# Constant products on TensorE in the first microseconds, and mask copies moved behind the casts of unit 7

## The chip, the cores and the metric

The kernel runs on one core of one Trainium2 chip. The metric is the device time of one execution in microseconds (us): the median over three runs. A separate execution was recorded by the hardware profiler; its span is the time from the first to the last instruction, and the remainder of its device time lies around that span.

## The reference

Windowed attention with four sink keys, followed by a two-layer block with a gated activation. There are 4 batches, 8 heads, 768 positions and 64 elements per head.

```python
scores = scale * np.matmul(q, k.transpose(0, 1, 3, 2))
is_sink = pos[None, :] < 4
in_window = (rel >= 0) & (rel < 128)          # rel = query - key
scores = np.where(is_sink | in_window, scores, -1e9)
a = softmax(scores)                           # over the keys
attn = np.matmul(a, v)
...
x = attn.transpose(0, 2, 1, 3).reshape(3072, 512)
h = x @ w_in                                  # 512 -> 2048
g = h * (1.0 / (1.0 + np.exp(-beta * h)))
return g @ w_out                              # 2048 -> 512
```

## The kernel before

**Units.** The attention is cut into 32 units. Unit n is one batch (n // 8), one pair of heads (n % 4) and one half of the sequence, 384 queries (n // 4 % 2). Four units in a row make one tile T of 384 tokens of `xT`, the input of the second part, transposed. A unit goes through these steps:

- its q, k and v are loaded as f32 into `stage` (function `load`; DMA issues on SyncE's queue, lines 379 and 390, for v of units 0 and 1 on ScalarE's);
- `cast` (lines 425 and 428) copies them to bf16 on GpSimd: q and k into one of three buffers `qk16`, v into `v_aug`, whose buffer is shared by units that are eight apart, with one part for each half;
- for units below 12, `transpose_in` (line 447) has TensorE transpose q and k, six products of 128x128, into a PSUM bank, and ScalarE or VectorE copies that to `qkT` (line 454). From unit 12 on a transposing DMA does it;
- `scores` (line 487) multiplies keys and queries into PSUM in two parts; ScalarE takes the exponential of each part into `E` (line 493); VectorE multiplies it with a mask of zeros and ones (`mask`, line 502). From unit 12 on the two parts are handled at once (lines 521, 528, and 537, which reads the tile `mask_all`);
- `attend` (lines 560 and 571) multiplies with v, `normalise` (lines 579 and 581) divides, and `transpose_out` (line 598, and the copy on line 602) puts the result into `xT`; for units below 12 on TensorE.

**The second part.** `hidden(i)`, i from 0 to 127 (tile T = i // 16, block m = i % 16 of 128 columns of `w_in`), makes four products of 128x384 (line 618), a tanh on ScalarE (line 626) and a gate on VectorE (line 639). `project` (line 646) multiplies the gated tile with `w_out`, in products of 128x512, and the results leave by ScalarE, SyncE's queue and DMA. The weights come in 16 pieces of 512 KB (`load_w`, line 409), which GpSimd casts to bf16 (`cast_w`, line 414).

**The order.** The program is first written down as a list of operations with what each reads and writes (`op`). `Prog.order` then places them: each operation has a planned duration `busy` and a planned delay `lag` until others see its result, and on each engine the operation comes next that could start first by that plan, the earlier written one among equals. At most 160 places ahead of the first unplaced operation of an engine are looked at. `emit` derives the semaphore waits from the order. On the chip each engine works through its list in that fixed order: an operation that has to wait holds everything behind it on its engine. The plan holds no slower start of TensorE: a product of n columns is planned at 2.5 + n / 2.4 ns.

**The start.** `constants` fills tiles: `ones` on VectorE, the identity and the masks `mask_a` and `mask_b` on GpSimd, zeros in `v_sink` on VectorE. Units 0 to 3 are then written one after the other (lines 692 to 701): `enter(n)` (transposes, the cast of unit n + 2, and in `enter(1)` also the casts of weight pieces 0 to 3 and two small DMA issues on GpSimd for the sink rows of v, line 689), scores, masks, `attend`, `normalise`, and `transpose_out` through PSUM bank `acc1`. After that come the first three products of `hidden(0)` and `hidden(1)`, into `acc0` and `acc1`, `transpose_out(3)`, and a loop over steps s from -6, in which hidden blocks are written among the steps of units 4 and up (`FIRST` gives each unit's first step).

**The masks that units from 12 on use.** `mask_all` is filled by six copies on GpSimd, written at step s = 16 (lines 763 to 773). They read only `mask_a` and `mask_b`, which are there early, so the plan is free to place them early. The cast of unit 7 is written at step s = -3.

Of the kernel before, what the change touches and what calls it, by code (L numbers as in the profile page):

```python
# [49 lines left out]
class Node:  # L50


    __slots__ = ("id", "eng", "items", "busy", "lag", "preds", "succs", "open", "ready", "done",
                 "place", "dma")

    def __init__(self, id, eng):
        self.id, self.eng = id, eng
        self.items = []
        self.busy = self.lag = 0.0
        self.preds = {}  # L60
        self.succs = []
        self.open = 0
        self.ready = self.done = 0.0
        self.place = None
        self.dma = None


class Prog:

# [28 lines left out]

        return Together()

    def op(self, eng, fn, r=(), w=(), x=(), dma=None, busy=100.0, lag=None, behind=None):
        if self.group is not None and self.group.eng == eng:
            node = self.group
        else:
            node = Node(len(self.nodes), eng)
            self.nodes.append(node)
        events = []

        def dep(ev, raw):
            if ev is None or ev[0] is node:
                return
            same = ev[0].eng == eng and ev[0].dma is None and dma is None
            node.preds[ev[0].id] = ev[0]
            if not same or (raw and eng != "pe"):
                events.append(ev)

        for t in r:
            dep(self.writer.get(t), True)  # L120
        for t in (*w, *x):
            dep(self.writer.get(t), False)
            for ev in self.readers.get(t, ()):
                dep(ev, False)
        if behind is not None:
            events.append((node, behind))
        me = (node, len(node.items))
        if dma is not None:
            self.dma_count[dma] = self.dma_count.get(dma, 0) + 16
            node.dma = (dma, self.dma_count[dma])  # L130
        node.items.append((fn, dma, events))
        node.busy += busy
        node.lag = busy if lag is None else lag
        for t in r:
            self.readers.setdefault(t, []).append(me)
        for t in (*w, *x):
            self.writer[t] = me
            self.readers[t] = []

    def order(self):  # L140

        for n in self.nodes:
            n.open = len(n.preds)
            for p in n.preds.values():
                p.succs.append(n)
        free = dict.fromkeys(self.ENGINES, 0.0)
        left = {e: [n for n in self.nodes if n.eng == e] for e in self.ENGINES}
        head = dict.fromkeys(self.ENGINES, 0)
        can = {e: [n for n in left[e] if n.open == 0] for e in self.ENGINES}
        placed = []  # L150
        dma_free = self.FIRST_DMA

        def best(e):
            q = left[e]
            while head[e] < len(q) and q[head[e]].place is not None:
                head[e] += 1
            if head[e] == len(q):
                return None
            last = q[min(head[e] + self.AHEAD[e], len(q) - 1)].id
            c = [n for n in can[e] if n.id <= last]  # L160
            if not c:
                return None
            n = min(c, key=lambda n: (max(n.ready, free[e]), n.id))
            return max(n.ready, free[e]), n

        while len(placed) < len(self.nodes):
            found = [(*b, e) for e in self.ENGINES if (b := best(e)) is not None]
            start, n, e = min(found, key=lambda f: (f[0], f[1].id))
            free[e] = start + n.busy
            if n.dma is None:  # L170
                n.done = start + n.busy + n.lag
            else:

                dma_free = max(dma_free, start + n.busy) + n.lag
                n.done = dma_free + 2000.0
            n.place = start
            can[e].remove(n)
            placed.append(n)
            for s in n.succs:
                s.open -= 1  # L180
                s.ready = max(s.ready, n.done if s.eng != e or n.dma else start + n.busy)
                if s.open == 0:
                    can[s.eng].append(s)
        return placed
# [64 lines left out]
def bass_streamingllm_window__then__act_swish_beta_kernel(  # L249
# [21 lines left out]
    def sb(name, shape, dtype):  # L271
        ctx.append(nc.sbuf_tensor(name, list(shape), dtype))
        return ctx[-1].__enter__()

    def ps(name, shape, dtype):
        ctx.append(nc.psum_tensor(name, list(shape), dtype))
        return ctx[-1].__enter__()
# [8 lines left out]
    ones = sb("ones", (128, 256), BF16)  # L286
# [6 lines left out]
    mask_all = sb("mask_all", (128, 2, 768), BF16)  # L293
    stage = {t: [sb(f"{t}_stage{z}", (128, 2, 6, D), F32) for z in range(4)] for t in "qkv"}
    qk16 = [sb(f"qk16_{z}", (128, 2, 3, 2, D), BF16) for z in range(NQK)]
    v_aug = [sb(f"v_aug{z}", (128, 6, 2, D1), BF16) for z in range(4)]
# [13 lines left out]
    acc = [ps(f"acc{z}", (128, NOUT), F32) for z in range(2)]  # L310
# [3 lines left out]
    op = P.op  # L314
# [5 lines left out]
    def act(n):  # L320
        return {"busy": 80.0 + 0.81 * n, "lag": 140.0}
# [43 lines left out]
    MASK_A, MASK_B = ["mask_a", "mask_a1"], ["mask_b0", "mask_b1"]  # L365


    def place(n):

        return n // 8, n % 4, n // 4 % 2, n % 4  # L370
# [108 lines left out]
    def scores(n, c, bank, name):  # L479
        _, _, half, pb = place(n)  # L480
        at = 0
        with P.together("pe"):
            for kb, qb, nq in CHUNKS[half][c]:
                w = 128 * nq
                for hh in range(2):
                    rows = slice(64 * hh, 64 * hh + 64)
                    op("pe", lambda e, at=at, w=w, kb=kb, qb=qb, hh=hh, rows=rows: e.matmul(  # L487
                        bank[:, hh, at:at + w], qkT[pb][rows, kb // 3, 1, kb % 3 * 128:kb % 3 * 128 + 128],
                        qkT[pb][rows, half, 0, qb % 3 * 128:qb % 3 * 128 + w], start=True, stop=True),
                       r=[("qkT", pb, half), ("qkT", pb, kb // 3)], w=[f"{name}{hh}"],  # L490
                       busy=50.0 + w / 4.8, lag=260.0)
                at += w
        op("act", lambda e: e.activation(E[n % 2][:, c, :, 0:at], bank[:, 0:2, 0:at], AF.Exp,  # L493
                                         bias=0.0, scale=SCALE),
           x=[f"{name}0", f"{name}1"], w=[("E", n % 2, c)], **act(768))
# [170 lines left out]
    for n in range(4):  # L666
        load(n, "act" if n < 2 else "sp")
    op("act", lambda e: e.dma_start(beta_stage[:, :], moe_beta.rearrange("(m p) -> m p", p=128)),
       w=["beta_stage"], dma="beta")
# [6 lines left out]
    cast(0)  # L676
    cast(1)

    def enter(n):
        transpose_in(n, *((tr_ps, "tr") if n % 2 == 0 else (acc[0], "acc0")), "act")  # L680
        if n + 2 < 6:
            cast(n + 2)
        if n == 1:
            for i in range(4):
                cast_w(i)
            for hh in range(2):
                rows = slice(HEAD1 * hh, HEAD1 * hh + NSINK)
                s = v[:, :, 0:NSINK, :].rearrange("b (g h) s d -> s h (b g) d", h=2)[:, hh]
                op("gp", lambda e, hh=hh, rows=rows, s=s: e.dma_start(v_sink[rows, :, hh, 0:D], s),
                   w=[("v_sink", hh)], r=["v_sink"], dma=f"s{hh}")  # L690

    for n in range(4):
        enter(n)
        scores(n, 0, s_ps, "s")
        scores(n, 1, h_ps, "h")
        mask(n, 0)
        mask(n, 1)
        attend(n)
        normalise(n)
        if n < 3:  # L700
            transpose_out(n, acc[1], "acc1", "act" if n else "dve")
    op("pe", lambda e: nc.tensor.transpose(acc[0][:, 0:16], beta_stage[:, :], ident32[0:16, 0:16]),
       r=["beta_stage", "ident32"], w=["acc0"])
    op("dve", lambda e: e.tensor_scalar(beta_half[:, :], acc[0][:, 0:16], 0.5, None, ALU.mult),
       x=["acc0"], w=["beta"])
# [11 lines left out]
    for s in range(-6, S_END + NM):  # L717
# [5 lines left out]
        for n, step in here:  # L723
            half = place(n)[2]
# [20 lines left out]
        if s in casts:  # L745
            n = casts[s]
# [16 lines left out]
        if s == NM:  # L763

            first = {0: (mask_a[:, :], MASK_A), 1: (mask_b[:, 128:512], MASK_B)}
            for half in range(2):
                op("gp", lambda e, half=half: e.tensor_copy(mask_all[:, half, 0:TT], first[half][0]),
                   r=first[half][1], w=[("mask_all", half, 0)], busy=300.0)
                for x, n in ((0, 1), (1, 2)):
                    at = TT + 128 * x  # L770
                    op("gp", lambda e, half=half, n=n, at=at: e.tensor_copy(
                        mask_all[:, half, at:at + 128 * n], mask_b[:, 0:128 * n]),
                       r=MASK_B, w=[("mask_all", half, 1)], busy=200.0)
        if s == FIRST[7] + 1:

            for x in (8, 9, 10, 11):
# [61 lines left out]
```

## Time and profile before

| what | value |
|---|---|
| time, median of three runs | 240.41 us (239.73 to 241.25) |
| the profiled execution, device time | 241.05 us |
| its span | 239.3 us |
| TensorE products, busy | 217.9 us, 1677 instructions |
| TensorE weight loads, busy | 118.2 us |
| VectorE, busy | 137.7 us |
| ScalarE, busy | 147.7 us |
| GpSimd, busy | 73.3 us |
| read from HBM, written to it | 27.30 MB, 6.29 MB |

In the profile PE is TensorE's products, PEld its weight loads, DVE is VectorE, ACT is ScalarE, POOL is GpSimd, SP is SyncE; a q behind an engine's name is its instruction queue, where DMAs are issued. A row of the timeline has its start and its length in us, the engine, the line of the kernel, the operation, the tiles written and read, their shapes and the number of instructions merged into the row; in brackets the idle time before it and what ended it. A product's recorded duration holds the time of passing through the array: products overlap, and the distance between two starts is what one costs in a row of many. The chain of waits is the work that ended last, followed back from the last instruction.

### The profile page before, as it was taken

What the parts mean: (1) busy time and instruction counts of PE and PEld (TensorE: products, weight loads), DVE (VectorE), ACT (ScalarE), POOL (GpSimd) and SP (SyncE); (2) the same over time, 40 slices, a digit from 0 to 9 for tenths busy, and PEclk for the clock granted to TensorE, in tenths of its full rate; (3) what the DMA queues carried; (4) which work ended last, traced back from release to release, by engine and by line L of the source; (5) the groups of instructions that cost most, each with busy time, mean ns of one, the idle gap of its engine ahead of it and who ended that gap; (6) DMA issues with size and microseconds to landing.
All of it is one profiled execution on the core that took longest, in us unless ns stands there. A gap on an engine that the chain in (4) does not pass through costs nothing.

```text
span 239.3 us, 4359 instructions
## 1 busy us (share of the span) xinstructions
PE 217.9 (91%) x1677; PEld 118.2 (49%) x1677; DVE 137.7 (58%) x262; ACT 147.7 (62%) x254; POOL 73.3 (31%) x134
## 2 busy tenths in 40 slices
PE   0567769799999999999999999999999999999994
PEld 0244435455545555554555555555555555555441
DVE  4066499859974565653676537664666656434300
ACT  2477487559852756765877667658767865554411
POOL 7989568529251133232223337000000000000000
PEclk9999999999999999999999999999999999999999
DMA  7999999899799999999999976512201022111022
GB/s 176 260 374 280 334 377 294 221 284 251 169 227 207 209 183 276 231 164 216 225 167 237 195 148 152 126 28 60 63 16 47 16 60 63 44 44 44 5 85 88
DMA packets 96084, 39.76 MB, mean 166 GB/s; under 512 B 82736, under 2 KB 88896, under 8 KB 96064
## 3 DMA queue, kind: packets, MB, share of 16 engines
q1 hardware_dynamic: 93888, 39.07, 71.0%
q10 hardware_dynamic: 1632, 0.40, 0.8%
q8 instruction: 13, 0.21, 0.4%
q0 software_dynamic: 544, 0.02, 0.2%
q14 instruction: 7, 0.06, 0.1%
HBM read 27.30 MB, written 6.29 MB: 140 GB/s over the span
## 4 chain that ended last, share of the span: by engine, by line
PE 81%; DVE 11%; ACT 4%; POOL 2%; issue 1%; ACTq 0%
PE acc L646 34%; PE h_ps L618 28%; PE s_ps L571 5%; DVE E L502 5%; PE acc L618 4%; PE s_ps L521 4%; ACT E L493 2%; DVE g L639 2%; DVE qkT L454 1%; PE h_ps L646 1%; PE s_ps L487 1%; PE s_ps L560 1%; DVE v_sink L335 1%; PE s_ps L469 1%; DVE o_norm L581 1%
## 5 line engine op out<-in xcount | busy, mean ns | idle before, releaser
L646 PE MATMUL acc<-w_out,g 128*128 128x512 bf16 x368 | 98.5, 380 | 0.0
L626 ACT ACTIVATE th<-h_ps,beta_half 128x384 f32<-128x384 f32 x104 | 59.3, 582 | 39.0 <-PE h_ps L618 37.6
L618 PE MATMUL h_ps<-xT,w_in 128*128 128x384 bf16 x416 | 80.1, 326 | 0.2 <-DVE g L639 0.2
L639 DVE SCALAR_TENSOR_TENSOR g<-th,h_ps 128x384 bf16<-128x384 f32 x104 | 56.3, 552 | 33.3 <-ACT th L626 31.9
L618 PEld LDWEIGHTS h_ps<-xT,w_in 128*128 128x128 bf16 x416 | 39.6, 98 | 30.9 <-DVE g L639 1.7
L646 PEld LDWEIGHTS acc<-w_out,g 128*128 128x128 bf16 x368 | 34.4, 98 | 33.4 <-issue 3.0
L537 DVE TENSOR_TENSOR E<-E,mask_all 128x1536 bf16<-128x1536 bf16 x20 | 19.7, 984 | 26.4 <-ACT E L528 26.4
L528 ACT ACTIVATE E<-s_ps 128x1536 bf16<-128x1536 f32 x20 | 29.0, 1449 | 7.5 <-PE s_ps L521 7.1
L425 POOL CAST qk<-q_stage 128x384 bf16<-128x384 f32 x32 | 18.8, 588 | 34.2 <-DMA qkT<-qk 17.9
L428 POOL CAST v_aug<-v_stage 128x384 bf16<-128x384 f32 x32 | 17.1, 546 | 36.8 <-PE s_ps L571 35.9
L571 PE MATMUL s_ps<-v_aug,E 128*128 128x65 bf16 x384 | 21.1, 199 | 3.2 <-DVE E L502 3.0
L571 PEld LDWEIGHTS s_ps<-v_aug,E 128*128 128x128 bf16 x384 | 18.1, 101 | 9.0 <-DVE E L502 4.1
L618 PE MATMUL acc<-xT,w_in 128*128 128x384 bf16 x96 | 20.2, 341 | 1.6 <-DVE g L639 1.3
L654 ACT ACTIVATE out_sb<-acc 128x512 f32<-128x512 f32 x23 | 13.6, 597 | 11.3 <-PE acc L646 10.8
L581 DVE TENSOR_TENSOR o_norm<-s_ps,rden 128x384 bf16<-128x384 f32 x32 | 17.8, 558 | 1.8
L626 ACT ACTIVATE th<-acc,beta_half 128x384 f32<-128x384 f32 x24 | 13.8, 585 | 7.9 <-PE acc L618 7.4
L425 POOL CAST qk<-k_stage 128x384 bf16<-128x384 f32 x32 | 17.6, 550 | 0.1
L493 ACT ACTIVATE E<-s_ps 128x768 bf16<-128x768 f32 x16 | 13.0, 812 | 4.9 <-PE s_ps L487 4.7
L639 DVE SCALAR_TENSOR_TENSOR g<-th,acc 128x384 bf16<-128x384 f32 x24 | 13.0, 548 | 2.8 <-ACT th L626 2.7
L447 PE MATMUL s_ps<-ident,qk 128*128 128x128 bf16 x60 | 6.3, 246 | 8.8 <-POOL qk L425 8.3
L502 DVE TENSOR_TENSOR E<-E,mask_b 128x768 bf16<-128x768 bf16 x16 | 13.5, 847 | 1.2 <-ACT E L493 0.9
L618 PEld LDWEIGHTS acc<-xT,w_in 128*128 128x128 bf16 x96 | 8.4, 102 | 8.0 <-DVE g L639 3.5
(58 smaller groups left out, 147.4 us busy)
## 6 DMA issues: line engine op xcount, KB each, us to landing
out_dram<-out_sb SPq DMA_DIRECT2D x24, 256.0 KB, 2.7
q_stage<-in_q_dram SPq DMA_DIRECT2D x28, 192.0 KB, 4.3
k_stage<-in_k_dram SPq DMA_DIRECT2D x28, 192.0 KB, 4.9
wst<-in_moe_w_in_dram SPq DMA_DIRECT2D x8, 512.0 KB, 6.8
wst<-in_moe_w_out_dram SPq DMA_DIRECT2D x8, 512.0 KB, 7.6
v_stage<-in_v_dram SPq DMA_DIRECT2D x16, 192.0 KB, 4.0
v_stage<-in_v_dram SPq DMA_DIRECT2D x28, 96.0 KB, 5.0
q_stage<-in_q_dram SPq DMA_DIRECT2D x8, 96.0 KB, 4.1
```

What stands on the lines that cost most here:

```text
L425: op("gp", lambda e, x=x, name=name: e.tensor_copy(qk16[z][:, x, :, :, :], view(name)), r=[(name + "_stage", pb, half, hh) for hh in range ...
L428: op("gp", lambda e: e.tensor_copy(v_aug[pb][:, 3 * half:3 * half + 3, :, 0:D], view("v")), r=[("v_stage", pb, half, hh) for hh in range(2 ...
L493: op("act", lambda e: e.activation(E[n % 2][:, c, :, 0:at], bank[:, 0:2, 0:at], AF.Exp, bias=0.0, scale=SCALE), x=[f"{name}0", f"{name}1"] ...
L502: op("dve", lambda e: e.tensor_tensor(E[n % 2][:, c, :, 0:w], E[n % 2][:, c, :, 0:w], m[:, first:first + w].unsqueeze(1).to_broadcast([128 ...
L528: op("act", lambda e: e.activation(E[z][:, :, :, :].rearrange("p c h x -> p c (h x)"), s_ps[:, :, :].rearrange("p (h b) x -> p h (b x)", h ...
L537: op("dve", lambda e: e.tensor_tensor(both, both, mask_all[:, half, :].unsqueeze(1).to_broadcast([128, 2, 768]), ALU.mult), r=[("E", z, 0) ...
L571: last=(x == len(kbs) - 1): e.matmul(av_ps[:, at + hh * D1:at + hh * D1 + D1], E[z][:, c, h2, col:col + 128], v_aug[pb][:, kb, hh, :], sta ...
L581: op("dve", lambda e: e.tensor_tensor(o_norm[o][:, :, :, :].rearrange("p m h d -> p (m h) d"), src[:, :, 0:D], rden[z][:, :].unsqueeze(2). ...
L618: op("pe", lambda e: e.matmul(bank, w_in16[:, c, m * 128:(m + 1) * 128], xT[:, c, T * TT:(T + 1) * TT], start=(c == 0), stop=(c == 3)), r= ...
L626: op("act", lambda e: e.activation(th[i % 3][:, :], bank, AF.Tanh, bias=0.0, scale=beta_half[:, m:m + 1]), x=[name], r=["beta"], w=[("th", ...
L639: op("dve", lambda e: e.scalar_tensor_tensor(g[T % 2][:, m, :], th[i % 3][:, :], 1.0, bank, ALU.add, ALU.mult), r=[("th", i % 3)], x=[name ...
L646: op("pe", lambda e: e.matmul(bank, g[T % 2][:, m, t * 128:(t + 1) * 128], w_out16[:, m, :], start=(m == 0), stop=(m == NM - 1)), r=[("g", ...
```

## The change

Four things are changed.

1. `keep_busy(count, busy, behind)` is new. It writes `count` products of `ones` with `ones` (weights 128x128, 256 columns) into PSUM bank `acc1`; nobody reads them. Fourteen are written before unit 0 and wait for `ones` alone. Behind the transposes of unit 0, seven more read the cast k of unit 0 and seven the cast k of unit 1, so that they wait for these casts. Three follow each `transpose_out` of units 0, 1 and 2. That makes 37 products.
2. Because they write `acc1`, they stand in one order with the other users of that bank: `transpose_out` of units 0 to 2 comes after the products written before it, the three products behind it come after the copy that empties the bank, and so does `hidden(1)`.
3. An operation can carry `give`: in the choice of the next operation on an engine it counts as that much later. The constant products carry 200 ns. Their planned durations are 215, 200, 160 and 120 ns.
4. The six copies into `mask_all` also read v of unit 7 as cast (`("v_aug", 3, 1)`), so that they stand behind that cast on GpSimd.

```diff
-    def op(self, eng, fn, r=(), w=(), x=(), dma=None, busy=100.0, lag=None, behind=None):
+    def op(self, eng, fn, r=(), w=(), x=(), dma=None, busy=100.0, lag=None, behind=None,
+           give=0.0):
...
         node.busy += busy
+        node.give = give
...
-            n = min(c, key=lambda n: (max(n.ready, free[e]), n.id))
+            n = min(c, key=lambda n: (max(n.ready, free[e]) + n.give, n.id))
             return max(n.ready, free[e]), n
...
     cast(0)
     cast(1)
 
+    def keep_busy(count, busy, behind=()):
+
+        for _ in range(count):
+            op("pe", lambda e: e.matmul(acc[1][:, 0:256], ones[:, 0:128], ones[:, :], start=True,
+                                        stop=True), r=["ones", *behind], w=["acc1"], busy=busy,
+               lag=260.0, give=200.0)
+
+
+    keep_busy(14, 215.0)
...
     for n in range(4):
         enter(n)
+        if n == 0:
+            keep_busy(7, 200.0, [("k16", 0)])
+            keep_busy(7, 160.0, [("k16", 1)])
         scores(n, 0, s_ps, "s")
...
             transpose_out(n, acc[1], "acc1", "act" if n else "dve")
+            keep_busy(3, 120.0)
...
             for half in range(2):
                 op("gp", lambda e, half=half: e.tensor_copy(mask_all[:, half, 0:TT], first[half][0]),
-                   r=first[half][1], w=[("mask_all", half, 0)], busy=300.0)
+                   r=[*first[half][1], ("v_aug", 3, 1)], w=[("mask_all", half, 0)], busy=300.0)
                 for x, n in ((0, 1), (1, 2)):
...
-                       r=MASK_B, w=[("mask_all", half, 1)], busy=200.0)
+                       r=[*MASK_B, ("v_aug", 3, 1)], w=[("mask_all", half, 1)], busy=200.0)
```

More of the change, by code (lines that the diff above doesn't have):

```diff
@@ L50 @@
 class Node:
-    __slots__ = ("id", "eng", "items", "busy", "lag", "preds", "succs", "open", "ready", "done",
+    __slots__ = ("id", "eng", "give", "items", "busy", "lag", "preds", "succs", "open", "ready", "done",
                  "place", "dma")
@@ L58, in __init__ @@
         self.items = []
-        self.busy = self.lag = 0.0
+        self.busy = self.lag = self.give = 0.0
         self.preds = {}
```

## The prediction

> **What bounds the kernel now.** I read the page first, then the windows by stage, the chain of waits, and the timelines of GpSimd and TensorE. From the page, the chain that ended last:
>
> ```profile
> span 239.3 us, 4359 instructions
> ...
> PE 81%; DVE 11%; ACT 4%; POOL 2%; issue 1%; ACTq 0%
> ```
>
> TensorE carries it, but not all the way. The windows (columns: length, then busy time and instructions of PE, PEld, DVE, ACT and POOL, clock, DMA share, GB/s) show two regimes:
>
> ```profile
> 27.60:45.00 17.40, 13.34 (x144) 7.43 (x142) 15.64 (x28) 13.67 (x24) 13.80 (x20) 1.00 1.00 314
> 45.00:60.00 15.00, 13.98 (x114) 7.99 (x114) 12.03 (x24) 10.26 (x22) 8.14 (x11) 1.00 1.05 265
> ...
> 65.00:236.00 171.00, 170.98 (x1264) 90.73 (x1262) 93.27 (x174) 105.59 (x175) 28.45 (x56) 1.00 0.63 126
> ```
>
> From 65 us on TensorE never stops, so the end lies a fixed amount of TensorE work behind that point. Whatever brings the first 65 us forward brings the end forward; the change touches only these. The start is a serial walk through units 0 to 3, on GpSimd first (timeline of POOL):
>
> ```profile
> 4.28 1.37 POOL L689 DMA_DIRECT2D v_sink<-in_v_dram  x2 [0.83 <-DVE v_sink L335]
> 5.64 0.52 POOL L767 COPY mask_all<-mask_a 128x384 bf16<-128x384 bf16 x1
> ...
> 7.12 0.63 POOL L771 COPY mask_all<-mask_b 128x128 bf16<-128x128 bf16 x2
> 7.71 0.50 POOL L425 CAST qk<-q_stage 128x384 bf16<-128x384 f32 x1
> ```
>
> The first cast starts at 7.71, right behind the mask copies, though its q, issued at 0.81, landed 3.1 us later, at 3.9. TensorE's first product follows at 8.26. And early products are slow (timeline of PE):
>
> ```profile
> 23.78 2.11 PE L618 MATMUL acc<-xT,w_in 128*128 128x384 bf16 x6
> ...
> 26.78 0.82 PE L447 MATMUL s_ps<-ident,qk 128*128 128x128 bf16 x6 [0.57 <-ACT xT L602]
> ...
> 29.19 0.51 PE L447 MATMUL s_ps<-ident,qk 128*128 128x128 bf16 x6
> 29.54 0.81 PE L618 MATMUL acc<-xT,w_in 128*128 128x384 bf16 x4
> ```
>
> Six transposes take 0.82 us at 26.78 and 0.51 at 29.19; in the chain six products of line 618 take 1.92 us at 23.97 (320 ns each), later four take 0.65 (162 ns). TensorE runs at half speed until about 27.6, although the clock column reads 1.00 throughout: the column doesn't show it, the durations do.
>
> **Masks.** Removed from before cast 0: six copies, 5.64 to 7.71, 2.07 us. What was queued behind them is the row of casts of units 0 to 3, all issued back to back until 13.8. By issue plus time to landing, q and k of unit 0 are there at 3.9 and 4.9, of unit 1 at 6.1 and 7.3 (its v at 8.1), of unit 2 at 8.3 and 8.8 (v 9.8), of unit 3 at 11.5 and 12.2 (v 13.0). So unit 0 gains 2.07, unit 1 1.9, unit 2 1.5, unit 3 nothing. That is enough: the chain reaches unit 3's transposes only at 15.5, 2.8 us after its k can be cast, and the shift at unit 0 is handed on through exponentials and masks (11.50, 15.52, 19.44, 21.23). I count 2.07; bounds 1.5 (unit 2's data) and 2.07.
>
> The copies land behind the cast of unit 7 (27.42 to 28.8), ahead of the casts of weight pieces 4 to 7 (28.78 on, each waiting 0.2 to 0.8 for its data). Those move by up to 2.1 us. Piece 4 serves block 8, which the chain starts at 42.6, so this is free unless the start gains more than 8 us. Nothing is issued to SyncE's queue from there but loads into freed weight buffers, which have 10 us and more of slack (the last w_out piece lands at 56.8, is used after 75). Units 12 on need the masks at about 90. The price is company for VectorE: a masking of 128x768 took 0.56 us at 15.52 and 1.20 at 11.50, with casts on GpSimd. Two microseconds of copies in a stretch where VectorE is 90% busy cost 0 to 0.6 (one masking drawn out from 0.56 to 1.20); I take 0.3. Maskings at 9 to 11 us may get that back, as GpSimd then waits for data.
>
> **The clock.** The trace of before has no product before 8.26, so when the speed rises is to be bounded. Two stretches give a clue. In 23.06 to 26.0 TensorE streamed almost without a break (12 small products at 54 ns, six at 320, three at 107: 2.9 us) and was fast from 27.6. In 15.2 to 23 it was busy some three quarters of the time by the records, which hold latency, and stayed slow. After 27.6 waits of up to 1.1 us (at 35.37) did not slow it again. Fourteen constant products at 213 ns (320 x 256/384) are 2.98 us, from about 1.3 (when `ones` is written) to 4.3, as dense as the stretch that worked. Should they not suffice, unit 0's transposes at 6.2 with two times seven more products make the stretch from 6.2 to about 10 dense again. Value: fast from 6 to 10 us. Bounds: fast at unit 0's first step, or as late as before, at 27.6.
>
> [...]
>
> Worth, from rows of the chain between 8 and 27.6, slow against fast: three transposes of unit 1, 0.50 to 0.34; scores of unit 0, 0.51 to 0.34; `attend` of units 0 and 1, 0.68 to about 0.40 each, of unit 3, 0.71 to 0.54 (the twelve at 148.79); transposes out of units 2 and 3, 0.16 each; six products of line 618, 1.92 to 0.97; unit 4's transposes, 0.84 to 0.50. Sum 0.16 + 0.17 + 0.56 + 0.17 + 0.32 + 0.95 + 0.34 = 2.67; with unit 0 partly slow 2.5.
>
> **Cost of the products.** The first 14 lie where TensorE has nothing to do. Of the 14 behind the casts of k, 3.0 us slow or 1.5 fast, TensorE's idle time between 8.2 and 15.2 (7.00 less 5.04 busy) covers 2.0: between the last transpose and the scores of unit 0 stands a copy of 0.80 us, and `give` keeps products back when something real is due within 200 ns of the plan. The nine behind the transposes out must wait for `acc1` to be emptied: by the rows the copies ended at 16.35, 20.48 and 23.78, 0.7 to 1.1 us behind the transposes. If the plan puts them later than that, they wait for nothing and cost 9 x 108 ns = 1.0 at most, inside waits of up to 1.2 us for VectorE. Bounds 0 to 3.7 (1.0 uncovered, three stalls of 0.9); I take 0.5, near the covered end, as the plan knows these waits and its exponentials and maskings are shorter than the real ones, so that real gaps are longer.
>
> **What is late next.** Shifted by about 4 us, unit 4's transposes fall at 22.8; its k lands at 19.7 and is cast by 21.2. Units 5 and 6 have as much room, unit 7 (k landed 26.6, transposed at 36.65) 8 us. Data takes nothing back.
>
> **The sum.** -2.07 - 2.5 + 0.3 + 0.5 = -3.8. The profiled execution, 241.05 with a span of 239.3, would come to 237.3; it ran 0.64 above the median of 240.41, so the forecast is 236.6. With every bound at its best (-2.07 - 2.67 - 0.5 for undisturbed maskings) 235.2, less 0.4 for scatter 234.8; with half the clock's worth and 1.0 more for products 238.9, so its own range is 234.8 to 238.6.
>
> **Rivals.** (1) The gain is half eaten: the speed rises late or falls back in the sparse steps of units 1 to 3, so the products cost 213 ns each, or the newly planned order of units 4 to 7, where VectorE is the bound, hands part back. For it: VectorE 15.64 of 17.40 us busy from 27.6. Against it: that work moves forward as a whole. Masks -2.07, clock -0.5, costs +1.3: 239.1. (2) Slower: the nine products behind the transposes out block TensorE's queue. ScalarE empties `acc1` of units 1 and 2 behind exponentials of 0.81, so a product placed too early holds `attend` or the next scores. Three stalls of 0.9 to 1.1, 1.0 for the uncovered slow products, each pushed through VectorE's masks to the next unit, +1.5 for casts of units 2 and 3 that find their data late, no gain from the clock, masks -2.07: 240.4 + 3.0 + 1.0 + 1.5 - 2.1 = 243.8. It decides once stalls and uncovered products exceed the 2.07 of the masks. Against it: the plan places these products by the copy's end.
>
> **Chances.** Forecast 0.60, rival 1 0.26, rival 2 0.14. Three runs of before spread over 1.5 us, so under 1% (2.4 us, to 238.0) tells nothing from no change. Of the forecast 0.55 and of rival 1 0.02 lie below 238.0: faster 0.57; same 0.31 (most of rival 1, the top of the forecast, the mildest of rival 2); slower 0.12. The range takes in the forecast and rival 1: 234.8 to 240.6.
>
> **What would show it.** First cast at 5.6; six transposes in 0.5 us and products of line 618 at 162 ns before 23 us; unit 4's transposes near 23 instead of 26.8; TensorE without a break from about 61. I am wrong if line 618 is still at 320 ns in its first six products, if a constant product waits for a copy with `attend` behind it, or if the shift at unit 4 is there and gone at 65.

## The result, and the profile after

| | before | changed |
|---|---|---|
| median of 20 runs each, in turn on one chip | 240.50 us | 238.41 us |
| ratio of the times | | 0.9898 (95%: 0.9871 to 0.9925) |
| recorded execution, device time | 241.05 us | 238.34 us |
| its span | 239.3 us | 236.6 us |

The change is worth about 2.4 us (240.5 x 0.0102). Ratios and runs listed below leave disturbed executions out, and medians don't; two recorded executions, of `e12_filled` and `e1_again`, were disturbed ones, so that only their first 27 us are read for times.

The page of the changed kernel, in the lines that answer to those of before (line numbers are 3 higher, and 13 to 17 higher behind the new function):

```profile
span 236.6 us, 4404 instructions
...
PEclk9997999999999999999999999999999999999999
...
PE 77%; DVE 10%; ACT 6%; DMA 3%; issue 2%; POOL 1%; SPq 0%; ACTq 0%
```

The timeline of GpSimd has the first cast where the copies of masks began:

```profile
4.28 1.37 POOL L702 DMA_DIRECT2D v_sink<-in_v_dram  x2 [0.84 <-DVE v_sink L338]
5.64 0.52 POOL L428 CAST qk<-q_stage 128x384 bf16<-128x384 f32 x1
```

And TensorE's timeline, where the chain leaves units 0 to 3:

```profile
21.05 1.15 PE L621 MATMUL acc<-xT,w_in 128*128 128x384 bf16 x3
21.99 0.79 PE L685 MATMUL acc<-ones 128*128 128x256 bf16 x3
22.61 0.65 PE L621 MATMUL acc<-xT,w_in 128*128 128x384 bf16 x3
...
24.00 0.51 PE L450 MATMUL s_ps<-ident,qk 128*128 128x128 bf16 x6 [0.57 <-ACT xT L605]
```

Unit 4's transposes start at 24.00 instead of 26.78, 2.78 us earlier, and the span is 2.7 shorter. But of the six products of hidden(0) and hidden(1) the first three still run at half speed (1.15 us for three, 320 ns from start to start), the last three at full speed (0.65), and three constant products stand between them. The chain of waits prices all three groups:

```profile
21.24 0.96 PE acc L621 x3
22.20 0.58 PE acc L685 x3
22.78 0.49 PE acc L621 x3
```

0.96 + 0.58 + 0.49 is 2.03 us, against 1.92 for the six at half speed in the chain of before. At this place the products took what the speed gave. Constant products stand on the chain earlier, too, among the first steps of units 0 to 2:

```profile
7.16 0.85 PE acc L685 x4
...
9.09 0.32 PE acc L685
...
9.73 0.85 PE acc L685 x4
...
10.90 0.43 PE acc L685 x2
...
14.48 0.39 PE acc L685 x2
```

With the 0.58 this is 3.42 us. It is not what leaving them out would save: where they stand, the chain of before went in large part through exponentials and maskings (4.2 us between 10.65 and 16.1), and in the masks-only run below, which has no constant products, the last nine products of `attend` of unit 0 start at 11.12, where the twelve start here.

What TensorE's clock did is told by windows of 3.41 us, the step in which the record's stretches come (6.83 at full speed from 12.35, 3.41 at half from 19.17; the columns: length, busy time and instructions of PE, PEld, DVE, ACT and POOL, granted clock, DMA share, GB/s). The changed kernel:

```profile
2.11:5.52 3.41, 2.35 (x12) 1.36 (x9) 1.64 (x3) 0.71 (x2) 2.42 (x6) 1.00 1.03 249
5.52:8.93 3.41, 2.71 (x19) 1.68 (x19) 0.00 (x0) 1.31 (x4) 2.72 (x7) 1.00 1.20 288
8.93:12.35 3.42, 3.42 (x33) 2.64 (x31) 1.86 (x4) 2.46 (x5) 2.22 (x5) 1.00 1.19 283
...
15.76:19.17 3.41, 2.11 (x29) 1.17 (x26) 3.36 (x6) 3.34 (x8) 2.67 (x4) 1.00 1.15 324
19.17:22.59 3.42, 3.07 (x25) 1.94 (x23) 1.97 (x5) 0.73 (x3) 3.42 (x6) 0.50 1.00 254
```

The clock column reads 1.00 from the first row on, but the transposes and scores up to 12.35 take the long times of before (three transposes 0.53 at 10.38, against 0.34 at 12.54): ahead of the first rise the column shows nothing of it. The rise comes at 12.35, behind a window in which TensorE was busy throughout (3.42 of 3.42). It falls at 19.17, behind a window with 2.11 us of work in 3.41, and the longest idle stretch in that window is 1.08 us. One window later it is back. So the speed was there from 12.3 to 19.2, while ScalarE and VectorE were busy nearly throughout (3.34 and 3.36 of 3.41 in the fourth row shown), and was missing for `attend` of unit 3 and the first three products of the second part, which stand on the chain.

### The profile page after: what moved, and what is told of

Its sections match the earlier page's. It is cut to its first block, busy times and chain, and to the rows that moved or that the text cites. A ratio compares the mean times of both kernels' runs of the same rounds, so it can differ in the third digit from the quotient of the medians.

```text
span 236.6 us, 4404 instructions
## 1 busy us (share of the span) xinstructions
PE 220.5 (93%) x1691; PEld 120.8 (51%) x1714; DVE 135.4 (57%) x262; ACT 147.1 (62%) x254; POOL 75.8 (32%) x134
## 4 chain that ended last, share of the span: by engine, by line
PE 77%; DVE 10%; ACT 6%; DMA 3%; issue 2%; POOL 1%; SPq 0%; ACTq 0%
PE acc L649 31%; PE h_ps L621 26%; PE s_ps L574 5%; PE acc L621 4%; DMA qkT<-qk 3%; PE s_ps L524 3%; DVE E L505 3%; DVE g L642 2%; ACT th L629 2%; ACT E L496 2%; DVE qkT L457 2%; PE acc L685 1%; PE h_ps L649 1%; PE s_ps L450 1%; PE s_ps L490 1%
## 5 line engine op out<-in xcount | busy, mean ns | idle before, releaser
L649 PE MATMUL acc<-w_out,g 128*128 128x512 bf16 x346 | 93.3, 380 | 1.2 <-issue 0.3
L428 POOL CAST qk<-q_stage 128x384 bf16<-128x384 f32 x32 | 17.6, 549 | 42.8 <-DMA qkT<-qk 39.7
L431 POOL CAST v_aug<-v_stage 128x384 bf16<-128x384 f32 x32 | 16.3, 521 | 24.3 <-PE s_ps L574 16.8
L574 PE MATMUL s_ps<-v_aug,E 128*128 128x65 bf16 x384 | 19.8, 196 | 1.9 <-DVE E L505 1.8
L621 PE MATMUL acc<-xT,w_in 128*128 128x384 bf16 x96 | 19.8, 333 | 1.8 <-DVE g L642 1.5
L574 PEld LDWEIGHTS s_ps<-v_aug,E 128*128 128x128 bf16 x384 | 17.6, 99 | 7.0 <-DVE E L505 2.5
L428 POOL CAST qk<-k_stage 128x384 bf16<-128x384 f32 x32 | 18.7, 585 | 1.6 <-DMA k_stage<-in_k_dram 1.1
L584 DVE TENSOR_TENSOR o_norm<-s_ps,rden 128x384 bf16<-128x384 f32 x32 | 17.8, 557 | 1.8
L505 DVE TENSOR_TENSOR E<-E,mask_b 128x768 bf16<-128x768 bf16 x16 | 11.3, 706 | 1.8 <-ACT E L496 1.6
L685 PE MATMUL acc<-ones 128*128 128x256 bf16 x37 | 9.1, 389 | 2.1 <-DVE ones L338 1.3
```

The lines of the kernel that those rows point to most:

```text
L428: op("gp", lambda e, x=x, name=name: e.tensor_copy(qk16[z][:, x, :, :, :], view(name)), r=[(name + "_stage", pb, half, hh) for hh in range ...
L431: op("gp", lambda e: e.tensor_copy(v_aug[pb][:, 3 * half:3 * half + 3, :, 0:D], view("v")), r=[("v_stage", pb, half, hh) for hh in range(2 ...
L505: op("dve", lambda e: e.tensor_tensor(E[n % 2][:, c, :, 0:w], E[n % 2][:, c, :, 0:w], m[:, first:first + w].unsqueeze(1).to_broadcast([128 ...
L574: last=(x == len(kbs) - 1): e.matmul(av_ps[:, at + hh * D1:at + hh * D1 + D1], E[z][:, c, h2, col:col + 128], v_aug[pb][:, kb, hh, :], sta ...
L584: op("dve", lambda e: e.tensor_tensor(o_norm[o][:, :, :, :].rearrange("p m h d -> p (m h) d"), src[:, :, 0:D], rden[z][:, :].unsqueeze(2). ...
L621: op("pe", lambda e: e.matmul(bank, w_in16[:, c, m * 128:(m + 1) * 128], xT[:, c, T * TT:(T + 1) * TT], start=(c == 0), stop=(c == 3)), r= ...
```

## The experiments

Three theories were set against each other. Theory 1: the masks make the gain, the products give about as much as they take. Theory 2: the clock makes it. Theory 3: the newly planned order makes it, whatever the products are.

**The masks alone** (run twice). The edit is part 4 of the change and nothing else:

```diff
-                   r=first[half][1], w=[("mask_all", half, 0)], busy=300.0)
+                   r=[*first[half][1], ("v_aug", 3, 1)], w=[("mask_all", half, 0)], busy=300.0)
...
-                       r=MASK_B, w=[("mask_all", half, 1)], busy=200.0)
+                       r=[*MASK_B, ("v_aug", 3, 1)], w=[("mask_all", half, 1)], busy=200.0)
```

> Only the copies of masks are moved behind the cast of unit 7; no constant products. The order on TensorE, VectorE, ScalarE and SyncE is that of before, so this is the masks' term alone. Theory 1 (the masks make the gain; the products give about as much as they take): first cast at 5.64, six products of line 618 still at 320 ns, unit 4's transposes 1.5 to 2.1 us earlier than 26.78, time 1.5 to 2.1 us below before (238.4 to 239.0). Theory 2 (the clock makes the gain): no more than 0.5 us below before, since units 2 and 3 wait for their data. Theory 3 (the newly planned order makes it): also no more than 0.5.

> The masks alone once more, for a narrower interval: theory 1 has 1.5 to 2.1 us below before (0.991 to 0.994) and the changed kernel 0.5 to 1.0 below that; theory 2 has it within 0.5 of before.

Measured: 0.9939 of before (0.9896 to 0.9982), and on another chip 0.9935 (0.9894 to 0.9976): 1.5 us both times. The lists of instructions of the other four engines are word for word those of before. In the first of the two records TensorE's timeline has

```profile
21.22 2.11 PE L618 MATMUL acc<-xT,w_in 128*128 128x384 bf16 x6
24.22 0.82 PE L447 MATMUL s_ps<-ident,qk 128*128 128x128 bf16 x6 [0.57 <-ACT xT L602]
```

Both groups are slow, and unit 4 is still 2.56 us ahead of before. Not all of this need be the masks': in this record the speed was up from 15.31 to 18.72, without any constant product, behind a window with 3.01 us of work. In the second record it did not rise before 26.31, and unit 4 starts at 25.08, 1.70 ahead of before. Theory 1 holds for the masks, theories 2 and 3 fail as the whole story.

**The products alone.** The changed kernel with `r=first[half][1]` and `r=MASK_B` as in before:

```diff
-                   r=[*first[half][1], ("v_aug", 3, 1)], w=[("mask_all", half, 0)], busy=300.0)
+                   r=first[half][1], w=[("mask_all", half, 0)], busy=300.0)
...
-                       r=[*MASK_B, ("v_aug", 3, 1)], w=[("mask_all", half, 1)], busy=200.0)
+                       r=MASK_B, w=[("mask_all", half, 1)], busy=200.0)
```

> All 37 constant products, the copies of masks where they were. Theory 1: within 0.7 us of before (239.8 to 241.2), since what the faster clock gives on the chain is taken by products that stand on it. Theory 2: 1.8 to 2.5 us below before. Theory 3: like the changed kernel, 2 us below, if the new order on TensorE is what counts.

Measured: 0.9961 (0.9928 to 0.9994), 0.9 us below before. The products do give something, by the point a little more than theory 1 allowed, and not what theory 2 asks. 1.5 + 0.9 is 2.4, the gain of the whole change. Its record has full speed from 13.2 to 33.66, so that all six products are fast (0.65 for three, twice) and unit 4 starts early:

```profile
24.86 0.51 PE L450 MATMUL s_ps<-ident,qk 128*128 128x128 bf16 x6 [0.57 <-ACT xT L605]
```

That is 1.92 ahead of before. The span is only 1.1 shorter (238.2): between unit 4 and the end 0.8 is gone. One window at half speed lies there, from 33.66 on, but that it took the 0.8 is not shown. The window ahead of that fall:

```profile
30.25:33.66 3.41, 1.76 (x24) 1.11 (x23) 3.38 (x8) 2.67 (x5) 2.13 (x3) 1.00 1.04 377
```

**The order alone.** The products keep their places and their planned durations, but have 2 columns:

```diff
-            op("pe", lambda e: e.matmul(acc[1][:, 0:256], ones[:, 0:128], ones[:, :], start=True,
+            op("pe", lambda e: e.matmul(acc[1][:, 0:2], ones[:, 0:128], ones[:, 0:2], start=True,
```

> The changed kernel with 2 instead of 256 columns in each constant product: the order of every engine's instructions is that of the changed kernel, but the products take next to no time and hardly keep TensorE busy. Theory 1: like the masks alone, 1.5 to 2.1 us below before, within 0.7 of the changed kernel. Theory 2: half speed until after 20 us and no better than 0.5 below before, plus what the masks give there. Theory 3: as fast as the changed kernel or faster, even if the masks alone are not.

Measured: 0.992 (0.9886 to 0.9954), 1.9 us below before. The speed rises at 23.28 in its record, so theory 2 has nothing to explain these 1.9 with. They are 0.4 more than the masks' 1.5, which the intervals don't tell from nothing; nor do they tell theory 1 from theory 3 here, the masks' run does. In this record unit 4 starts at 24.19, without any speed ahead of 23.28. That is 2.59 ahead of before, and 0.9 more than in the second record of the masks alone, likewise slow up to there; whether this is the order or the scatter of single executions is not shown. The changed kernel's 24.00 is 0.19 earlier: by these two records, this is all that its speed, less its products' time, had won by then.

**Without the first fourteen.** The call is taken out:

```diff
-    keep_busy(14, 215.0)
```

> The changed kernel without the fourteen products that wait for nothing but the constant tile. My prediction's step (the first block may raise the speed by itself, or help to): products of line 450 slow until later than in the changed kernel, 0.3 to 1.0 us slower than it. Against it (the speed rises only after the stretch of TensorE work from 9 to 12.3, as the profile of the changed kernel has it): the same time as the changed kernel within 0.5 us, with the rise between 9 and 13.

Measured: 0.9966 (0.9929 to 1.0002), 1.6 us slower than the changed kernel by the ratios, from different chips; the second series of the changed kernel, below, has an interval that overlaps with this one. By the point the first block counts for more than either expectation had; that it counts is not shown, nor how: in this record the speed rises at 11.26, no later than in the changed kernel, and then is at half from 18.1 to 24.9, two windows instead of one.

**Without the nine behind the transposes out.**

```diff
-            keep_busy(3, 120.0)
```

> The changed kernel without the nine products that follow the transposes out of units 0 to 2. Theory A (they only stand on the chain: in the changed kernel's chain the last three take 0.58 us ahead of the last products of hidden(0) and hidden(1)): 0.3 to 0.8 us faster than the changed kernel. Theory B (they keep the speed up): the granted clock falls to half earlier or for longer than 3.4 us in the recorded execution, and the kernel is 0.3 to 1.0 slower than the changed one.

Measured: 0.9883 (0.9843 to 0.9924). By the point it is 0.4 us faster than the changed kernel, and the intervals overlap. Theory B's sign is in the record: half speed from 17.8 to 24.7, two windows, so that all six products of hidden(0) and hidden(1) are slow (2.11 at 21.19) and unit 4 starts at 24.19. No cost of that can be seen: the three products that would have stood in between (0.58) are gone too. This record also shows the first block raising the speed by itself, at 4.18, and TensorE losing it at 7.60 behind a window with 1.39 us of work.

**The speed held through units 2 and 3.** Twelve more products into the other bank:

```diff
+    for _ in range(12):
+        op("pe", lambda e: e.matmul(acc[0][:, 0:256], ones[:, 0:128], ones[:, :], start=True,
+                                    stop=True), r=["ones"], w=["acc0"], busy=120.0, lag=260.0,
+           give=200.0)
```

> The changed kernel with twelve more constant products, into the bank acc0, free to run behind the transpose of beta (15.8 us in the changed kernel) until hidden(0). If the fall to half speed at 19.2 in units 2 and 3 is what the changed kernel lacks against my forecast: no fall in the recorded execution, the six products of hidden(0) and hidden(1) at 162 ns, 0.5 to 1.5 us faster than the changed kernel and less scatter between runs. Rival (the products cost as much TensorE time as the speed gives back): within 0.4 us of the changed kernel or slower, without the fall.

Measured: 0.987 (0.983 to 0.9911), by the point 0.7 us below the changed kernel, with overlapping intervals; its six runs lie within 2.2 us. The record has no fall after 10.82, all six products at 162 ns, and unit 4's transposes at 22.25, which is 4.5 us ahead of before:

```profile
0.58:3.99 3.41, 2.69 (x13) 1.95 (x14) 2.52 (x9) 1.49 (x2) 2.45 (x10) 1.00 0.59 158
3.99:7.40 3.41, 1.39 (x13) 0.65 (x10) 0.00 (x0) 0.36 (x1) 3.12 (x6) 1.00 1.05 277
7.40:10.82 3.42, 3.31 (x23) 2.20 (x23) 1.45 (x2) 3.08 (x7) 2.33 (x5) 0.50 1.27 213
...
17.64:21.06 3.42, 2.92 (x40) 2.31 (x41) 2.74 (x7) 1.75 (x6) 3.09 (x4) 1.00 1.10 270
```

The borders lie elsewhere than in the changed kernel, so the rows can't be compared one by one. But wherever a window of 3.41 us is laid that starts between 13 and 19 us, this record has at least 2.39 us of work in it, and the changed kernel's goes down to 1.75; no fall came behind a window with more than 2.31 in any record here. Its span is 235.7, though, 3.6 below before: 0.9 of the 4.5 is lost behind unit 4. Behind 62 us TensorE itself waits 0.6 us, in two places, for transposing DMAs of q and k for units from 12 on (engine and line, what it waited for, us in total, times, longest):

```profile
PE s_ps L472 <- DMA qkT<-qk: 0.6, 2, 0.4
```

**A longer first block**, `keep_busy(22, 215.0)` in place of 14.

```diff
-    keep_busy(14, 215.0)
+    keep_busy(22, 215.0)
```

> Twenty-two constant products ahead of unit 0 in place of fourteen, so that they last from 1.3 to about 6.0 us, up to the first transposes. My theory now (a stretch of 3.4 us has to be filled nearly whole; fourteen products in 2.98 us fill none): the speed rises between 4.7 and 8.2, unit 0's transposes and scores are fast, 0.3 to 0.8 us faster than the changed kernel. Rival (speed in units 0 and 1 is worth nothing, because exponentials, maskings and the arrival of data set the pace): within 0.3 of the changed kernel, though the speed rises early.

Measured: 0.9866 (0.9809 to 0.9922), from three runs. The speed rises at 6.12, as expected, and unit 0 and 1 are fast; it falls at 19.8 for one window, and unit 4 starts at 23.91, 0.09 earlier than in the changed kernel. This does not show that speed in units 0 and 1 is worth nothing:

```profile
20.28 1.15 PE L621 MATMUL acc<-xT,w_in 128*128 128x384 bf16 x3
...
21.86 1.16 PE L621 MATMUL acc<-xT,w_in 128*128 128x384 bf16 x3
```

The first three products start 0.77 earlier than in the changed kernel, and the stretch at half speed, 0.6 later there, takes in all six. The second record of the changed kernel, below, has all six slow as well (1.15 and 1.16 for three), with the speed from 9.63 on: its first three start at 20.57 and its unit 4 at 24.10. Against that one, 3.5 us more of speed won 0.2 to 0.3 in these records, which is near the rival. The time is too uncertain to add to that.

**Both, without the nine** (twenty-two ahead, twelve into `acc0`, no `keep_busy(3, 120.0)`), and the same with the copies of masks back in front. The first differs from the changed kernel by

```diff
-    keep_busy(14, 215.0)
+    keep_busy(22, 215.0)
...
-            keep_busy(3, 120.0)
...
+    for _ in range(12):
+        op("pe", lambda e: e.matmul(acc[0][:, 0:256], ones[:, 0:128], ones[:, :], start=True,
...
```

> The changed kernel with the constant products put elsewhere: twenty-two ahead of unit 0, the fourteen behind the casts of k, twelve into acc0 behind the transpose of beta, and none behind the transposes out of units 0 to 2. If the speed is held from unit 0 on and the products stand beside other work, it has what my forecast counted: 3.0 to 4.5 us below before and 0.5 to 2.0 below the changed kernel. Rival (exponentials, maskings and data bound units 0 to 3 whatever TensorE does): within 0.5 us of the changed kernel.

> The same products, but the copies of masks ahead of unit 0's first cast as in before: the term of the clock by itself, where it is held. By my forecast's term (2.5 less 0.5 for the products): 1.5 to 2.5 us below before. If the products' half of the change was small because the speed was not held: the same. If it was small because TensorE's speed is worth little in units 0 to 3: 0.3 to 1.2 below before, although six products of line 621 take 162 ns each.

Measured, with the masks moved: 0.9865 (0.9796 to 0.9933), from three runs: 3.2 us below before, with 1.6 to 4.9 left open, so that the rival is not excluded. The speed rises at 6.74 and is held, and unit 4 starts 0.8 ahead of the 22.8 that my forecast had:

```profile
19.92 0.66 PE L621 MATMUL acc<-xT,w_in 128*128 128x384 bf16 x3
20.64 0.65 PE L621 MATMUL acc<-xT,w_in 128*128 128x384 bf16 x3
22.03 0.51 PE L450 MATMUL s_ps<-ident,qk 128*128 128x128 bf16 x6 [0.57 <-ACT xT L605]
```

With the masks in front: 0.9928 (0.9899 to 0.9957), 1.7 us below before, and unit 4 at 24.95 in its record, 1.83 ahead of before, though the speed was away from 9.43 to 12.85. That is the clock's term by itself, with products placed elsewhere: 1.7 by the point, inside the 1.5 to 2.5 that the forecast's term asks, against 0.9 for the products of the change; the intervals of the two overlap, and this one goes down to 1.0, so that the 0.3 to 1.2 of the other expectation is not excluded. No version is shown to beat the changed kernel: four of them lie at 0.9865 to 0.9883 with intervals that reach into its own.

**The changed kernel again**, unchanged.

> The changed kernel once more, beside the next three on the same chip: 1.0% below before, 0.987 to 0.993. If the place in time of the half-speed stretches is what scatters it, its runs spread over 3 us and more, and a second recorded execution has the rise and the fall at other times than 12.3 and 19.2.

Measured: 0.9913 (0.9877 to 0.9948) on another chip; the runs behind the ratio spread over 3.4 us (237.03 to 240.46). The second record has the rise at 9.63 and the fall at 19.87, so the stretches do sit elsewhere in each execution. On the first chip the times can be set beside the mean granted clock of each run (a window at half speed in 236.6 us is 3.41 / 2 / 236.6, 0.007; the time ahead of the first rise isn't in it):

```text
1.000          236.09 235.84 236.55
0.992 to 0.993 238.34 238.32 239.05 238.91 238.48 239.12 238.89
0.985 to 0.986 238.24 238.18 237.32 237.68 236.99 238.55
0.977 to 0.978 238.83 238.66
```

The three runs that never fell back average 236.2, 4.3 below before; those with one window at half speed 238.7. But those with two average 237.8, less than those with one, and on the second chip the run at 1.000 took 240.02. So this is a pointer and not a law.

**The first cast earlier still.** GpSimd's two DMA issues are made to wait for the cast of unit 3:

```diff
-                op("gp", lambda e, hh=hh, rows=rows, s=s: e.dma_start(v_sink[rows, :, hh, 0:D], s),
-                   w=[("v_sink", hh)], r=["v_sink"], dma=f"s{hh}")
+                op("gp", lambda e, hh=hh, rows=rows, s=s: e.dma_start(v_sink[rows, :, hh, 0:D], s),
+                   w=[("v_sink", hh)], r=["v_sink", ("v_aug", 3, 0)], dma=f"s{hh}")
```

> The changed kernel with GpSimd's two DMA issues for the sink rows of v (4.28 to 5.64) behind the cast of unit 3, so that nothing stands ahead of unit 0's first cast. First cast at about 4.0 instead of 5.64, as its data lands at 3.9. If the start is handed on as it was with the masks: 0.5 to 1.0 us faster than the changed kernel. If from here on the data of units 1 and 2 decides (q and k of unit 1 land at 6.1 and 7.3, its cast is at 7.0 and 7.4 already): within 0.3 us.

Measured: 0.9951 (0.9911 to 0.9992), by the point some 1.3 us slower than the changed kernel, which neither expectation had; against the second series of that kernel it is 0.9, with overlapping intervals. The first cast is at 3.88. But the two issues now stand at 13.69 to 15.05, the casts of weight pieces 0 to 3 behind them find all their data there and run without a gap, and a masking beside them takes 3.52 us (timelines of VectorE and GpSimd):

```profile
14.95 3.52 DVE L505 TENSOR_TENSOR E<-E,mask_a 128x768 bf16<-128x768 bf16 x1
```

```profile
13.69 1.36 POOL L702 DMA_DIRECT2D v_sink<-in_v_dram  x2 [0.74 <-DVE o_norm L584]
15.04 4.32 POOL L417 CAST w_in<-wst 128x1024 bf16<-128x1024 f32 x4
```

A masking that takes 0.56 at 14.21 takes 3.52 at 14.95, and unit 4 starts at 26.12. The speed is not the reason: it is away from 20.46 to 27.29 and all six products are slow (1.15 and 1.16 for three), but that is so in the second record of the changed kernel as well, where unit 4 starts at 24.10.

## Why the prediction was right, and which term was off

**The direction and the sum.** Faster, and 238.4 lies in the range, but 1.8 us above the forecast of 236.6. It lies near the upper end of the forecast's own part of the range, and this end has a slip: "half the clock's worth and 1.0 more for products" gives 238.9, and the text goes on with 238.6. By the mark that I had set for a change that can be told from none, 238.0, the median stays short, and the ratio just reaches the 1%. So the mechanism of the masks was right, and the size of the gain was not.

**Masks.** Counted at 2.07 less 0.3 for company to VectorE, 1.8; measured 1.5 in both series, with intervals of 1 us to either side. The mechanism is shown: same order on the other engines, the first cast at 5.64, and unit 4 earlier by 1.70 in a record in which the speed rose only after that. That units 2 and 3 wait for their data was no loss.

**Clock.** This is the term that was mis-sized: 2.5, net 2.0 behind the products' 0.5; the products alone brought 0.9. The 2.5 takes unit 0 as partly slow, 0.17 below the 2.67, and no run shows that term: in both records of the changed kernel unit 0's transposes and scores were as slow as in before (0.94 and 0.95 us for six transposes, 0.95 in before; 0.50 and 0.53 for the two parts of its scores in all three), and in `e12_filled`, with the speed from 6.74, the scores took 0.34 and 0.33. The step that failed is "fast from 6 to 10 us", and on to the end. The rise came at 12.35 in one record and at 9.63 in the other. And as waits of up to 1.1 us behind 27.6 had not slowed it again, I took it that the speed stays; it fell in both records, at 19.17 and 19.87, and the longest wait in the windows ahead was 1.08 and 1.23 us. The runs here speak for the work in a window rather than the longest wait: in the first record of the masks alone it fell at 18.72, behind a window with 2.27 us of work and no wait above 0.37; and filled up, as in `e9_twelve_more`, the same stretch stayed fast. The row that I leaned on shows how near it was, had I added it up; before, around its rise and in its sparse stretch:

```profile
20.80:24.21 3.41, 2.16 (x29) 1.78 (x27) 2.17 (x5) 1.97 (x5) 3.41 (x7) 1.00 1.16 280
24.21:27.63 3.42, 2.85 (x16) 1.66 (x15) 0.56 (x1) 0.48 (x1) 1.02 (x3) 1.00 1.09 315
34.45:37.87 3.42, 2.07 (x25) 1.35 (x26) 3.38 (x8) 2.39 (x5) 2.38 (x3) 1.00 1.08 373
```

At 2.07 it held, in the changed kernel at 2.11 it fell: the work of units 2 and 3 lies where these records have both. In the changed kernel's record a window that starts between 13 and 19 us holds anything from 1.75 to 3.1 us of work, by where its borders lie; that these decide is the likely reading and was not tried. The fall hit the products of line 621, the largest item of the 2.5 (0.95): three of the six in the first record, all six in the second.

Where the speed was held up to unit 4, its worth there was about what I had counted. Against `e5_two_columns`, slow up to 23.28 (24.19), unit 4 is 1.94 earlier in `e9_twelve_more` and 2.16 in `e12_filled`; with the masks in front it is 1.92 and 1.83 earlier than in before (`e2_products_only`, `e14_filled_masks_first`). In the changed kernel it is 0.19 and 0.09.

In the traces the stretches of one speed behind the first rise last 211.63 us in before, and 6.83, 3.41 and 215.04 in the changed kernel, which is 62, 2, 1 and 63 times 3.413, and the borders lie elsewhere in each execution: the first rise is at 27.63, at 12.35 and, in the second record of the changed kernel, at 9.63. For the longer first block I had it as my theory that a stretch of 3.4 us has to be filled nearly whole and that fourteen products fill none. That holds for the changed kernel's two records, with rises behind 3.42 and 3.41 us of work, and not for two others: the same fourteen products raised the speed at 3.99 (`e9_twelve_more`) and 4.18 (`e4_without_nine`), with 2.69 and 2.88 us of work in the window.

**Products.** Counted at 0.5, with TensorE's idle time for most of the fourteen and "inside waits" for the nine. In the record 3.42 us of constant products stand on the chain, 0.58 of it from the last three. What this cost is not shown. Taking the nine out neither won nor lost measurably; they took time on the chain, and without them the record has half speed for two windows instead of one. Neither was in the prediction.

**"Data takes nothing back."** This holds for the first units and not to the end. In before the chain of waits has no DMA in it; in the changed kernel DMA has 3% of it, 4.86 us at 107.96 and 2.81 us at 144.83, transposing DMAs of q and k for units from 12 on, and between 140 and 152 us TensorE is no longer without a break,

```profile
140.00:152.00 12.00, 11.47 (x97) 6.11 (x98) 8.25 (x16) 9.14 (x20) 5.40 (x10) 1.00 0.87 156
```

where before it was busy 11.98 of 12. ScalarE waits there 0.9 us for such DMAs; the second record of the changed kernel has no break there (12.00). In `e9_twelve_more`, 4.5 us ahead at unit 4, DMA has 11% of the chain:

```profile
PE 66%; DVE 12%; DMA 11%; SPq 4%; ACT 3%; issue 1%; POOL 1%; POOLq 0%; ACTq 0%
```

So "from 65 us on TensorE never stops" was true of before, and with the start brought forward these DMAs can come onto the path: they have 12% of the chain in `e4_without_nine`, and none of it in `e2_products_only`. The waits of TensorE itself are short, 0.6 us in `e9_twelve_more` and 0.3 in `e4_without_nine`. That the shift at unit 4 (2.78) and the shorter span (2.7) agree in the changed kernel's record is in part luck: `e2_products_only` has 1.92 and 1.1, `e14_filled_masks_first` 1.83 and 0.6. Each is one execution, and the runs of one kernel spread over 3 us.

**Rivals.** The first (gain half eaten, 239.1) came nearest, by one of its two mechanisms: the speed falls back in the sparse steps of units 1 to 3. The second (constant products blocking the queue) shows in the chain, as told, and in one stall of the three: at 14.48 two constant products have waited 0.77 us for VectorE's copy out of `acc1`, with scores of unit 2 and `attend` behind them, one of the signs that I had named for being wrong. It cost next to nothing, as those scores wait for ScalarE's copy into `qkT`, which ends at 14.67, and start at 14.81.

## What to carry to other kernels

Look for the place where TensorE's products stand on the chain before adding constant ones that keep it fast (here six of line 621 start 320 ns apart when slow, 162 when fast); count the work per window, 3.41 us in these records, up to that place, wherever the window's borders may lie, and look at what stands on the chain behind it. Filling the stretch from a bank that is not in use held the speed here in two records; that it makes the kernel faster than the plain change is not shown. Look first at what stands ahead of the first useful instruction on each queue: six small copies that nobody needed for 80 us cost 1.5 us, by the point more than the 37 constant products won (0.9). A move on one queue changes who is beside whom: what comes late runs in a block, and a VectorE instruction beside a block of GpSimd's casts took most of the block's length here (3.52 of 4.32 us, against 0.56 just ahead of it).

## What the runs showed of the hardware

- The granted clock of the profile reads 1.00 until its first change, although products run at half speed: 320 ns against 162 for 128x384 before 27.6 us in the kernel before. Read the start from durations.
- In the records here the speed rose behind windows of 3.41 us with 2.69 us or more of recorded work on TensorE, but not behind every such window (2.71 in the changed kernel, 3.16 in before, from 17.39 on). It fell behind windows with 1.2 to 2.3 and held behind all with more, behind some down to 2.0 and once at 1.76 (`e12_filled`, from 146.69 on). Recorded work holds more than the distance between starts (the six products of line 618 start 320 ns apart and are recorded as 2.11 us, so that the last one takes some 0.5). The two ranges overlap and are marks, no thresholds.
- In `e8_vsink_later` one masking of 128x768 took 0.56 us at 14.21, while GpSimd issued DMAs, and 3.52 at 14.95, beside four weight casts of GpSimd without a gap (4.32 us for the four; the median of one in before is 1.04). That is 3.4 times the 1.04, though by the record the masking starts 0.09 us ahead of the first cast. Why it takes that long is not shown.
